# Sliding-window decode attention with an MLP: w4's first rows in eight loads, w3 in two, one more V quad moving

## The chip, the cores and the metric

The kernel runs on one core of one Trainium2 chip. The metric is the device time of one execution in microseconds (us); the time before is 194.92 us, the median of three runs. The profile is one execution of the same program, taken by the hardware profiler.

Engines: TensorE (PE; its weight loads are PEld), VectorE (DVE), ScalarE (ACT), GpSimd (POOL) and SyncE (SP). SP computes nothing; it issues the loads here. Sixteen DMA engines move the data.

## What is computed

Cut to what matters, for eight sequences of one token each:

```
x = A_x
def A(x):                                   # x: layer norm of A_x
    q = (x @ wq)                            # 32 heads of 128
    k = k_cache[:, :, SK - W:, :]           # W = 2048 of 8192 places, 8 kv heads
    v = v_cache[:, :, SK - W:, :]
    p = softmax(q k^T / sqrt(128))
    return (p v) @ wo
h = x + A(layernorm(x))
def Bf(y):                                  # y: layer norm of h
    x1 = y + 0                              # the token shift is zero for one token
    return x1 + gelu(layernorm(x1) @ w3) @ w4
out = h + Bf(layernorm(h))
```

wq and wo are 4 MB each in bf16, the windows of K and V 64 MB together, w3 (512 x 1792) and w4 (1792 x 512) 1.8 MB each. B_w1, B_w2 and B_x have no part in the result for one token, and no kernel here loads them.

## The kernel before

**The stream of loads.** SP issues all large loads through one helper, `dma` (L192 to L195; the instruction itself is at L194). The order is written out in `loads` (L282 to L289): wq, then for each sequence b ("row" b below, 0 to 7) two quads of K and, two rows behind, two quads of V, a quad being four kv heads, 2 MB; then four loads of wo, one of w3 and four of w4. K and V land in `ring`, eight slots of 16 KB in each of 128 partitions; a load waits until the quad that had its slot is used up. wo takes over the space of wq (`wbig`), w3 the ring's slot 0 and w4 slot 1 (`W3S`, `W4S`); their waits, `w_free`, are for the last transposes of K's quads in these slots. Each load raises a semaphore by 16, one step per DMA engine.

**Attention, row by row.** K is transposed on PE (L314), copied by ACT and DVE (L323, L325), multiplied with q (L334), and the softmax follows (L349 to L403). The product with V is made in quads, w = 2b + j for row b and half j; `i` counts quarter quads, i // 4 = w. `pe_PV` (L415) has two forms. In `moving` V is the moving operand, 4 matmuls of 512 columns for each i into one PSUM bank; after the fourth, DVE picks each head's own part in four instructions into `acc` (L446, L449), and `finish(w)` (L453) adds the parts with one matmul of `sum_f` (L456) and scales the result into `oT_all` (L412). In `held` V is the stationary operand, 16 matmuls of 16 columns for each i into `O_ps` (L430), and the result only needs scaling. Quads below NV = 14 are moving; the two quads of row 7 (w = 14 and 15) are held. `bank` gives quads 11 to 13 banks of their own. `turn` (L510) and `pv` (L515) fix where in PE's order the quarter quads and their `finish` stand.

**The end.** `reorder` (L486) brings the heads into wo's order, `pe_wo` (L499) multiplies with the four loads of wo, each behind its semaphore. Then h, its mean and variance (L598 to L612) and `uT`; `pe_w3` (L617) makes y = w3^T u, hidden index on partitions, in chunks of 128: chunks 0 to 7 into `y_ps[0]`, 8 to 13 into `y_ps[1]`, four matmuls each; `w4_chunks` says which rows of w4, and so which columns of w3, a chunk has. DVE scales y (L647), ACT applies gelu (L649), and `pe_w4` (L658, through `rows`, L652, matmuls at L654) adds h, as f_hi and f_lo, and the product with w4, group by group behind w4's four semaphores. ACT and DVE copy the result, SP stores it (L687).

The loads of w3 and w4 before:

```
584             B_w3.rearrange("(a p r) f -> p a (r f)", a=2, r=2), sem_w3, w_free[0])
...
587         w4_rows, w4_chunks = ((0, 4), (512, 4), (1024, 4), (1536, 2)), {}
...
593             dma(SP, w4_sb[:, lo:lo + r, :].rearrange("p r n -> p (r n)"),
594                 B_w4[f0:f0 + 128 * r, :].rearrange("(p r) n -> p (r n)", r=r), sem, w_free[1] if lo == 0 else None)
```

The first three loads of w4 bring 512 rows each, four neighbouring rows (4 KB) to each of 128 partitions; the fourth brings 256 rows, two to each.

Of the kernel before, what the change touches and what calls it, by code (L numbers as in the profile page):

```python
# [6 lines left out]
dt = mybir.dt  # L7
# [60 lines left out]
def bass_sequential_preLN__sliding_block_cached__mixer_s_mlp__decode_kernel(  # L68
# [23 lines left out]
    with es:  # L92
# [32 lines left out]
        w4_sb = ring[:, W4S, 0:FC * D].rearrange("p (k n) -> p k n", k=FC)  # L125
# [42 lines left out]
        g_x = sb([128, FC * B], dt.float32, "g_x")  # L168
        gT = sb([128, FC * B], dt.bfloat16, "gT")
# [18 lines left out]
        sem_x, sem_wq, sem_w3, sem_out = (S(n) for n in ("sem_x", "sem_wq", "sem_w3", "sem_out"))  # L188
# [111 lines left out]
        NV = 2 * (NB - 1)  # L300
# [104 lines left out]
        e_acc, e_oT = {}, {}  # L405

        def bank(w):
            return O_ps[:, :] if w < NV - 3 else kbank[(2, 3, 0)[w - NV + 3]]
# [6 lines left out]
        def pe_PV(i):  # L415
# [11 lines left out]
            def held(e):  # L427
                for c in range(16):
                    n = 16 * r + c
                    ins = e.matmul(O_ps[:, 16 * j:16 * (j + 1)], ring[:, s, n * DH:(n + 1) * DH],  # L430
                                   pT_sb[:, b % NB3, c, 64 * j + 16 * r:64 * j + 16 * (r + 1)],
                                   start=(n == 0), stop=(n == NCQ - 1))
                return ins

            if w >= NV:
                e_PV[i] = PE.op(held, landed(("v", b, j), r), e_pT[b, 3], e_acc[NV - 4])
                taken["v", b, j] = e_PV[i]
                return
            free = [e_xp[0]] if w == 0 else [e_acc[w - 1]] if w < NV - 3 else [e_lo[NG - 1], e_hi[NG - 1], e_lo[NG - 2], e_hi[NG - 2]]
# [46 lines left out]
        def reorder():  # L486
# [9 lines left out]
            e = PE.op(f, e_scale[LAST, 1], e_lo[NG - 1], e_hi[NG - 1], e_lo[NG - 2], e_hi[NG - 2])  # L496
# [17 lines left out]

        def pv(i):  # L515
            w = i // 4
            if i % 4 == 0 and 0 < w < NV - 3:
                finish(w - 1)
            pe_PV(i)
            if i % 4 == 0 and w == NV - 3:  # L520
                finish(w - 1)
            if i % 4 == 0 and w >= NV:
                for v in ((NV - 3, NV - 2), (NV - 1,))[w - NV]:
                    finish(v)
            if i == NG - 1:
                for j in range(2):
                    scale(LAST, j, O_ps[:, 16 * j:16 * (j + 1)], e_PV[i])
# [40 lines left out]
        for l in loads:  # L568
# [14 lines left out]
        dma(SP, w3_sb.rearrange("p (a r) f -> p a (r f)", a=2),  # L583
            B_w3.rearrange("(a p r) f -> p a (r f)", a=2, r=2), sem_w3, w_free[0])

        FH = 8
        w4_rows, w4_chunks = ((0, 4), (512, 4), (1024, 4), (1536, 2)), {}
        w4_ends = []
        for (f0, r), sem in zip(w4_rows, sem_w4):
            lo = len(w4_chunks)  # L590
            for i in range(r):
                w4_chunks[lo + i] = slice(f0 + i, f0 + 128 * r, r)
            dma(SP, w4_sb[:, lo:lo + r, :].rearrange("p r n -> p (r n)"),
                B_w4[f0:f0 + 128 * r, :].rearrange("(p r) n -> p (r n)", r=r), sem, w_free[1] if lo == 0 else None)
            w4_ends.append(lo + r)
        assert len(w4_chunks) == FC
# [20 lines left out]
        def pe_w3(lo, hi, *waits):  # L617
            def f(e):
                for fc in range(lo, hi):
                    n, f = divmod(fc, FH)  # L620
                    for kc in range(KC):
                        ins = e.matmul(y_ps[n][:, f * B:(f + 1) * B], w3_sb[:, kc, w4_chunks[fc]],
                                       uT[:, kc * B:(kc + 1) * B], start=(kc == 0), stop=(kc == KC - 1))
                return ins
            return PE.op(f, *waits)
        e_y = [pe_w3(0, FH, e_u, (sem_w3, 16), e_scale[LAST, 1]), pe_w3(FH, FC)]
# [12 lines left out]
        def bcf(t, n):  # L639
            a = t[:, :]  # L640
# [3 lines left out]
        for n in range(2):  # L644
            fn = (FH, FC - FH)[n]
            cs = slice(n * FH * B, (n * FH + fn) * B)
# [78 lines left out]
```

## Time and profile before

| | |
|---|---|
| runs | 194.76, 194.92, 195.19 us; median 194.92 |
| the profiled execution | 194.77 us; span from its first to its last instruction 193.0 us |
| PE, DVE, ACT busy | 81%, 53%, 43% of the span |
| read from HBM | 79.18 MB, 410 GB/s over the span |
| chain that ended last, by engine | DMA 56%, PE 33%, DVE 8% |
| SP's issues of w3 and w4 | five, from 158.79 to 175.24 us |
| clock granted to PE | full from 122.7 to 173.9 us, half from then on |

How to read the views. The page cuts the span into 40 equal slices of 4.8 us; a digit is the busy share of an engine in tenths, "DMA" the mean busy share of the 16 DMA engines, "GB/s" what they moved. The chain of waits goes back from the last instruction, at each step to what released it; a line has its start, its length and what it was. A table of stretches gives busy time and number of instructions per engine (PE, PEld, DVE, ACT, POOL), the granted clock, the DMA share and GB/s. A line of the timeline has start, length, engine, source line, operation, out<-in, shapes and number, and in brackets how long the engine stood idle before and what ended it. Besides these views the trace holds every step of every load's semaphore and one record for each DMA packet with its start, duration, size and queue.

### The profile page before, as it was taken

The numbers are of one execution on the slowest core, as the hardware profiler recorded it, in microseconds if no ns is written. First come the engines' busy times: TensorE is split into PE (matmuls) and PEld (weight loads), VectorE is DVE, ScalarE is ACT, GpSimd is POOL, SyncE is SP. The second block draws the span as 40 slices with busy tenths as digits, with TensorE's granted clock in tenths as the row PEclk, the third lists the DMA queues.
The fourth block names the chain that finished last, engine by engine and source line by source line (L and its number), as shares of the span: only waits on it lengthen the run. The fifth ranks groups of instructions, "written<-read, shape, count | busy, mean of one in ns | idle before, by whom it ended". The sixth has DMA issues, their size and how long they took to land.

```text
span 193.0 us, 4835 instructions
## 1 busy us (share of the span) xinstructions
PE 155.7 (81%) x2145; PEld 102.9 (53%) x2145; DVE 102.8 (53%) x256; ACT 82.7 (43%) x98; POOL 32.5 (17%) x40
## 2 busy tenths in 40 slices
PE   0028989889949999999789985999999798777753
PEld 0014767667736566566456643656565543347751
DVE  7702656456542665664756563464765735962051
ACT  5002866947822554464345442454445421430041
POOL 8000000350610080008000800044005200000000
PEclk9999999999996999999999998799999999995555
DMA  6999999999999999999999999999999999999981
GB/s 219 435 435 428 431 428 414 425 431 423 431 435 435 431 428 428 435 431 419 428 424 435 421 431 435 425 435 431 426 428 431 435 425 428 421 412 420 427 353 65
DMA packets 6740, 79.49 MB, mean 412 GB/s; under 512 B 688, under 2 KB 704, under 8 KB 2496
## 3 DMA queue, kind: packets, MB, share of 16 engines
q1 hardware_dynamic: 6704, 79.18, 96.8%
q8 instruction: 17, 0.28, 0.5%
q14 instruction: 3, 0.02, 0.0%
q10 hardware_dynamic: 16, 0.01, 0.0%
HBM read 79.18 MB, written 0.01 MB: 410 GB/s over the span
## 4 chain that ended last, share of the span: by engine, by line
DMA 56%; PE 33%; DVE 8%; issue 1%; SPq 1%; ACT 1%; ACTq 0%
DMA ring<-in_A_k_cache_dram 40%; PE kT_ps L314 13%; DMA ring<-in_B_w_dram 9%; PE O_ps L422 8%; DMA wbig<-in_A_wq_dram 6%; PE S_ps L334 4%; DVE acc L449 3%; PE S_ps L258 2%; DVE P_sb L371 1%; PE sm L456 1%; PE sm L381 1%; DVE iota_f L449 1%; DVE acc L446 1%; PE sm L400 1%; SPq L194 1%
## 5 line engine op out<-in xcount | busy, mean ns | idle before, releaser
L323 ACT ACTIVATE kT_sb<-kT_ps 128x1024 bf16<-128x1024 bf16 x64 | 65.2, 1024 | 66.4 <-PE kT_ps L314 66.4
L314 PE MATMUL kT_ps<-ident_p,ring 128*128 128x128 bf16 x1024 | 69.5, 222 | 7.9 <-DMA ring<-in_A_k_cache_dram 7.9
L325 DVE COPY kT_sb<-kT_ps 128x1024 bf16<-128x1024 bf16 x64 | 44.2, 691 | 51.7 <-PE kT_ps L314 51.6
L314 PEld LDWEIGHTS kT_ps<-ident_p,ring 128*128 128x128 bf16 x1024 | 59.2, 99 | 20.9 <-issue 10.2
L371 POOL TENSOR_TENSOR P_sb<-P_sb,mask_b 128x512 bf16<-128x512 bf16 x28 | 28.2, 1041 | 117.6 <-ACT P_sb L363 108.8
L422 PE MATMUL O_ps<-ring,pT_sb 128*64 128x512 bf16 x176 | 27.7, 402 | 0.0
L334 PE MATMUL S_ps<-kT_sb,qwin 128*32 128x512 bf16 x256 | 26.3, 395 | 0.0
L334 PEld LDWEIGHTS S_ps<-kT_sb,qwin 128*32 128x32 bf16 x256 | 6.8, 93 | 19.7 <-issue 17.7
L381 PE MATMUL sm<-ident_s,P_sb 128*128 128x128 bf16 x128 | 12.3, 219 | 3.8 <-DVE pT_sb L391 1.3
L391 DVE COPY pT_sb<-sm 128x512 bf16<-128x512 bf16 x28 | 11.7, 417 | 2.3 <-PE sm L381 2.3
L381 PEld LDWEIGHTS sm<-ident_s,P_sb 128*128 128x128 bf16 x128 | 8.1, 97 | 7.7 <-issue 3.7
L422 PEld LDWEIGHTS O_ps<-ring,pT_sb 128*64 128x64 bf16 x176 | 6.5, 109 | 4.6 <-issue 1.7
L449 DVE SCALAR_TENSOR_TENSOR acc<-O_ps,own_f,acc 128x128 f32<-128x128 f32 x24 | 8.4, 351 | 0.9
L363 ACT ACTIVATE P_sb<-S_ps,negcol 128x512 bf16<-128x512 f32 x8 | 5.5, 687 | 7.7 <-DVE negcol L362 7.7
L258 PE MATMUL S_ps<-wbig,xlnT 128*32 128x512 bf16 x32 | 3.6, 629 | 5.3 <-DMA wbig<-in_A_wq_dram 5.3
L456 PE MATMUL sm<-sum_f,acc 128*128 128x16 f32 x20 | 4.1, 281 | 3.6 <-DVE acc L449 1.6
L422 PE MATMUL kT_ps<-ring,pT_sb 128*64 128x512 bf16 x48 | 6.9, 388 | 0.0
L244 PE MATMUL sm<-ident_b,xln_b 8*128 8x8 bf16 x4 | 0.3, 174 | 7.5 <-DVE xln_b L217 7.5
L628 ACT ACTIVATE s<-vsum,eps 128x8 f32<-128x8 f32 x1 | 0.3, 302 | 13.9 <-DVE vsum L611 13.9
L345 DVE TENSOR_REDUCE mcol<-S_ps 128x1 f32<-128x512 f32 x8 | 5.5, 687 | 1.2 <-PE S_ps L334 1.2
L456 PEld LDWEIGHTS sm<-sum_f,acc 128*128 128x128 f32 x20 | 3.2, 200 | 5.1 <-DVE acc L449 2.6
L258 PEld LDWEIGHTS S_ps<-wbig,xlnT 128*32 128x32 bf16 x32 | 1.2, 138 | 6.8 <-issue 6.8
(113 smaller groups left out, 105.7 us busy)
## 6 DMA issues: line engine op xcount, KB each, us to landing
ring<-in_A_k_cache_dram SPq DMA_DIRECT2D x16, 2048.0 KB, 26.7
ring<-in_A_v_cache_dram SPq DMA_DIRECT2D x16, 2048.0 KB, 20.2
wbig<-in_A_wq_dram SPq DMA_DIRECT2D x1, 4096.0 KB, 12.2
wbig<-in_A_wo_dram SPq DMA_DIRECT2D x4, 1024.0 KB, 24.7
ring<-in_B_w_dram SPq DMA_DIRECT2D x1, 1792.0 KB, 26.9
ring<-in_B_w_dram SPq DMA_DIRECT2D x3, 512.0 KB, 17.7
ring<-in_B_w_dram SPq DMA_DIRECT2D x1, 256.0 KB, 17.8
x_sb<-in_A_x_dram ACTq DMA_DIRECT2D x1, 8.0 KB
```

Of the source, the lines that this page charges most:

```text
L258: ins = e.matmul(S_ps[u][32 * t:32 * (t + 1), :], xlnT[:, kc, :], wq_v[:, kc, lo:lo + 512], start=(kc == 0), stop=(kc == KC - 1), tile_pos ...
L314: ins = e.matmul(kT_ps[i % 2][:, c * 128:(c + 1) * 128], ring[:, s, n * DH:(n + 1) * DH], ident_p[:, :], is_transpose=True)
L323: e_lo[i] = AC.op(lambda e: e.activation(kT_sb[:, i % NKT, 0:1024], kT_ps[i % 2][:, 0:1024], ACT.Copy), e_Tlo[i], e_QK.get(i - NKT))
L325: e_hi[i] = DV.op(lambda e: e.tensor_copy(kT_sb[:, i % NKT, 1024:2048], kT_ps[i % 2][:, 1024:2048]), e_Thi[i], e_QK.get(i - NKT))
L334: ins = e.matmul(S_ps[b % 2][32 * h:32 * (h + 1), :], qwin[:, b, 4 * j + h, w0:w0 + 32], kT_sb[:, i % NKT, :].rearrange("p (c h k) -> p h ...
L345: e_max[b] = DV.op(lambda e: e.tensor_reduce(mcol[:, :], S_ps[b % 2][:, :], AX.X, ALU.max), e_QK[8 * b + 7], e_mT.get(b - 1))
L371: e_sp[b, r] = eng.op(lambda e, r=r, pb=pb, mb=mb: e.tensor_tensor(P4_sb[:, 128 * r:128 * (r + 1), :], pb, mb, ALU.mult), e_exp[b], e_PT.g ...
L381: ins = e.matmul(pT_ps[:, x * 128:(x + 1) * 128], P4_sb[:, 32 * c:32 * (c + 1), :].rearrange("p k h -> p (k h)"), ident_s[:, :], is_transp ...
L391: e_pT[b, r] = DV.op(lambda e: e.tensor_copy(dst, pT_ps[:, :]), e_PT[b, r], free)
L422: ins = e.matmul(bank(w)[64 * t:64 * (t + 1), :], pT_sb[:, b % NB3, c, 64 * j:64 * (j + 1)], ring[:, s, :].rearrange("p (a c d) -> p c a d ...
L449: e = DV.op(lambda e, own=own, src=src, dst=dst: e.scalar_tensor_tensor(dst, src, own, dst, ALU.mult, ALU.add), e)
L456: e_oT[w] = PE.op(lambda e: e.matmul(oT_ps[:, hh], acc[w % 3][:, :], sum_f[:, :], start=True, stop=True), e_acc[w], e_sum, small[0])
```

## The change

- **w4.** The first 512 rows go into partitions 0 to 63, eight neighbouring rows (8 KB) to each partition, by eight loads g = 0 to 7; load g brings the partitions g, g + 8, ... g + 56. All eight raise one semaphore, which is waited for at 128. The other three loads stay as they were. So w4 has 18 chunks instead of 14: eight of 64 rows (`FH` = 8 stays the border between the two banks of y) and ten of 128. `w4_sb` starts right behind w3 in the two slots of the ring, and all loads of w4 wait for `w_free[1]`.
- **w3.** Two loads of 256 rows, each with a semaphore. `pe_w3` runs first over all 18 chunks with the first half's rows (2 matmuls for each), then over chunks 0 to 7 and 8 to 17 with the second's.
- **w4's product.** The chunks of 64 rows use 64 partitions of gT and w4. `pe_fin` also waits for the scale of the last quad, which now has its result in the bank that `pe_fin` writes.
- **Row 7.** NV becomes 15: quad 14 is moving, into `O_ps`, and has its DVE instructions and a `finish`; quad 15 stays held, into `S_ps[1]`, and no longer waits for quad 10's DVE work. `at` and `late` write out where each `finish` stands: quad 11's goes from i = 56 to i = 54, quad 14's comes after i = 63, and `reorder` waits for it.

```
--- before.py
+++ after.py
...
-        w4_sb = ring[:, W4S, 0:FC * D].rearrange("p (k n) -> p k n", k=FC)
+        w34 = ring[:, W3S:W4S + 1, :].rearrange("p s n -> p (s n)")
+        w4_sb = w34[:, KC * F:KC * F + (FC + 4) * D].rearrange("p (k n) -> p k n", k=FC + 4)
...
-        g_x = sb([128, FC * B], dt.float32, "g_x")
-        gT = sb([128, FC * B], dt.bfloat16, "gT")
+        g_x = sb([128, (FC + 4) * B], dt.float32, "g_x")
+        gT = sb([128, (FC + 4) * B], dt.bfloat16, "gT")
...
-        sem_x, sem_wq, sem_w3, sem_out = (S(n) for n in ("sem_x", "sem_wq", "sem_w3", "sem_out"))
+        sem_x, sem_wq, sem_out = (S(n) for n in ("sem_x", "sem_wq", "sem_out"))
+        sem_w3 = [S(f"sem_w3{i}") for i in range(2)]
...
-        NV = 2 * (NB - 1)
+        NV = 2 * NB - 1
...
         e_acc, e_oT = {}, {}
+        OWN = {NV - 4: 2, NV - 3: 3, NV - 2: 0}
 
         def bank(w):
-            return O_ps[:, :] if w < NV - 3 else kbank[(2, 3, 0)[w - NV + 3]]
+            return kbank[OWN[w]] if w in OWN else O_ps[:, :]
...
                     n = 16 * r + c
-                    ins = e.matmul(O_ps[:, 16 * j:16 * (j + 1)], ring[:, s, n * DH:(n + 1) * DH],
+                    ins = e.matmul(S_ps[1][:, 0:16], ring[:, s, n * DH:(n + 1) * DH],
                                    pT_sb[:, b % NB3, c, 64 * j + 16 * r:64 * j + 16 * (r + 1)],
                                    start=(n == 0), stop=(n == NCQ - 1))
                 return ins
...
-                e_PV[i] = PE.op(held, landed(("v", b, j), r), e_pT[b, 3], e_acc[NV - 4])
+                e_PV[i] = PE.op(held, landed(("v", b, j), r), e_pT[b, 3])
                 taken["v", b, j] = e_PV[i]
                 return
-            free = [e_xp[0]] if w == 0 else [e_acc[w - 1]] if w < NV - 3 else [e_lo[NG - 1], e_hi[NG - 1], e_lo[NG - 2], e_hi[NG - 2]]
+            if w in OWN:
+                free = [e_lo[NG - 1], e_hi[NG - 1], e_lo[NG - 2], e_hi[NG - 2]]
+            else:
+                free = [e_xp[0]] if w == 0 else [e_acc[max(v for v in e_acc if v not in OWN)]]
             e_PV[i] = PE.op(moving, landed(("v", b, j), r), e_pT[b, r], *free)
...
-            e = PE.op(f, e_scale[LAST, 1], e_lo[NG - 1], e_hi[NG - 1], e_lo[NG - 2], e_hi[NG - 2])
+            e = PE.op(f, e_scale[LAST, 0], e_scale[LAST, 1], e_lo[NG - 1], e_hi[NG - 1], e_lo[NG - 2], e_hi[NG - 2])
...
+        at = {4 * (w + 1): (w,) for w in range(NV - 5)}
+        late = {4 * NV - 16: (NV - 5,), 4 * NV - 6: (NV - 4,), 4 * NV - 4: (NV - 3,), 4 * NV: (NV - 2,), NG - 1: (NV - 1,)}
+
         def pv(i):
-            w = i // 4
-            if i % 4 == 0 and 0 < w < NV - 3:
-                finish(w - 1)
+            for w in at.get(i, ()):
+                finish(w)
             pe_PV(i)
-            if i % 4 == 0 and w == NV - 3:
-                finish(w - 1)
-            if i % 4 == 0 and w >= NV:
-                for v in ((NV - 3, NV - 2), (NV - 1,))[w - NV]:
-                    finish(v)
             if i == NG - 1:
-                for j in range(2):
-                    scale(LAST, j, O_ps[:, 16 * j:16 * (j + 1)], e_PV[i])
+                scale(LAST, 1, S_ps[1][:, 0:16], e_PV[i])
+            for w in late.get(i, ()):
+                finish(w)
 
...
         w_free = [taken[quads[n - NS]] for n in (len(quads), len(quads) + 1)]
-        dma(SP, w3_sb.rearrange("p (a r) f -> p a (r f)", a=2),
-            B_w3.rearrange("(a p r) f -> p a (r f)", a=2, r=2), sem_w3, w_free[0])
-
-        FH = 8
-        w4_rows, w4_chunks = ((0, 4), (512, 4), (1024, 4), (1536, 2)), {}
+        for a, sem in enumerate(sem_w3):
+            dma(SP, w3_sb[:, 2 * a:2 * (a + 1), :].rearrange("p r f -> p (r f)"),
+                B_w3[256 * a:256 * (a + 1), :].rearrange("(p r) f -> p (r f)", r=2), sem, w_free[0])
+
+        w4_rows, w4_chunks = ((0, 64, 8), (512, 128, 4), (1024, 128, 4), (1536, 128, 2)), []
         w4_ends = []
-        for (f0, r), sem in zip(w4_rows, sem_w4):
+        for (f0, parts, r), sem in zip(w4_rows, sem_w4):
             lo = len(w4_chunks)
-            for i in range(r):
-                w4_chunks[lo + i] = slice(f0 + i, f0 + 128 * r, r)
-            dma(SP, w4_sb[:, lo:lo + r, :].rearrange("p r n -> p (r n)"),
-                B_w4[f0:f0 + 128 * r, :].rearrange("(p r) n -> p (r n)", r=r), sem, w_free[1] if lo == 0 else None)
-            w4_ends.append(lo + r)
-        assert len(w4_chunks) == FC
+            w4_chunks += [(parts, slice(f0 + i, f0 + parts * r, r)) for i in range(r)]
+            dst = w4_sb[0:parts, lo:lo + r, :].rearrange("p r n -> p (r n)")
+            rows_in = B_w4[f0:f0 + parts * r, :].rearrange("(p r) n -> p (r n)", r=r)
+            step = 128 // parts * 4 if parts < 128 else 1
+            for g in range(step):
+                dma(SP, dst[g::step], rows_in[g::step], sem, w_free[1])
+            w4_ends.append((len(w4_chunks), 16 * step))
+        FH = w4_ends[0][0]
+        NCH = len(w4_chunks)
...
-        def pe_w3(lo, hi, *waits):
+        def pe_w3(half, lo, hi, *waits):
             def f(e):
                 for fc in range(lo, hi):
-                    n, f = divmod(fc, FH)
-                    for kc in range(KC):
-                        ins = e.matmul(y_ps[n][:, f * B:(f + 1) * B], w3_sb[:, kc, w4_chunks[fc]],
-                                       uT[:, kc * B:(kc + 1) * B], start=(kc == 0), stop=(kc == KC - 1))
+                    parts, rows_of = w4_chunks[fc]
+                    n, f = (0, fc) if fc < FH else (1, fc - FH)
+                    for kc in (2 * half, 2 * half + 1):
+                        ins = e.matmul(y_ps[n][0:parts, f * B:(f + 1) * B], w3_sb[:, kc, rows_of],
+                                       uT[:, kc * B:(kc + 1) * B], start=(kc == 0 and f == 0), stop=(kc == KC - 1),
+                                       skip_group_check=True)
                 return ins
             return PE.op(f, *waits)
-        e_y = [pe_w3(0, FH, e_u, (sem_w3, 16), e_scale[LAST, 1]), pe_w3(FH, FC)]
+        pe_w3(0, 0, NCH, e_u, (sem_w3[0], 16), e_scale[LAST, 1], e_acc[NV - 2])
+        e_y = [pe_w3(1, 0, FH, (sem_w3[1], 16)), pe_w3(1, FH, NCH)]
...
-        def bcf(t, n):
-            a = t[:, :]
+        def bcf(t, n, ps):
+            a = t[ps, :]
             return bass.AP(tensor=a.tensor, offset=a.offset, ap=[a.ap[0], [0, n], [1, B]])
 
         e_gT = []
         for n in range(2):
-            fn = (FH, FC - FH)[n]
-            cs = slice(n * FH * B, (n * FH + fn) * B)
-            e = DV.op(lambda e, n=n, cs=cs, fn=fn: e.tensor_tensor(v3(g_x[:, cs]), v3(y_ps[n][:, 0:fn * B]), bcf(r2, fn),
-                                                                   ALU.mult), e_y[n], e_r2)
-            e_gT.append(AC.op(lambda e, cs=cs: e.activation(gT[:, cs], g_x[:, cs], ACT.Gelu_apprx_tanh), e))
+            fn = (FH, NCH - FH)[n]
+            ps, cs = slice(0, w4_rows[n][1]), slice(n * FH * B, (n * FH + fn) * B)
+            e = DV.op(lambda e, n=n, ps=ps, cs=cs, fn=fn: e.tensor_tensor(
+                v3(g_x[ps, cs]), v3(y_ps[n][ps, 0:fn * B]), bcf(r2, fn, ps), ALU.mult), e_y[n], e_r2)
+            e_gT.append(AC.op(lambda e, ps=ps, cs=cs: e.activation(gT[ps, cs], g_x[ps, cs], ACT.Gelu_apprx_tanh), e))
...
-                    ins = rows(e, [gT[:, fc * B:(fc + 1) * B]] * KC,
-                               [w4_sb[:, fc, cols[nb]] for nb in range(KC)],
-                               stop=(fc == FC - 1))
+                    p = slice(0, w4_chunks[fc][0])
+                    ins = rows(e, [gT[p, fc * B:(fc + 1) * B]] * KC,
+                               [w4_sb[p, fc, cols[nb]] for nb in range(KC)],
+                               stop=(fc == NCH - 1))
...
-        PE.op(pe_fin, e_fin, e_exp[LAST])
-        pe_w4(0, w4_ends[0], (sem_w4[0], 16), e_gT[0])
-        pe_w4(w4_ends[0], w4_ends[1], (sem_w4[1], 16))
-        pe_w4(w4_ends[1], w4_ends[2], (sem_w4[2], 16), e_gT[1])
-        e_z = pe_w4(w4_ends[2], w4_ends[3], (sem_w4[3], 16))
+        PE.op(pe_fin, e_fin, e_exp[LAST], e_scale[LAST, 1])
+        for n, (hi, count) in enumerate(w4_ends):
+            e_z = pe_w4(w4_ends[n - 1][0] if n else 0, hi, (sem_w4[n], count), e_gT[min(n, 1)])
```

## The prediction

> **What bounds the kernel now.** I read the 40 slices first, to see which resource is full, then the chain of waits, then stretches of the tail.
>
> ```profile
> PE   0028989889949999999789985999999798777753
> DMA  6999999999999999999999999999999999999981
> GB/s 219 435 435 428 431 428 414 425 431 423 431 435 435 431 428 428 435 431 419 428 424 435 421 431 435 425 435 431 426 428 431 435 425 428 421 412 420 427 353 65
> ```
>
> Transfers are at a ceiling of 435 GB/s in nearly every slice; only the last but one falls to 353. The chain of waits says what ends last:
>
> ```profile
> 171.72 17.66 DMA ring<-in_B_w_dram
> 189.37 0.04 issue
> 189.42 0.60 PE S_ps L654 x12
> 190.02 0.01 issue
> 190.03 0.41 PE S_ps L654 x6
> 190.44 0.02 issue
> 190.47 0.31 ACT P_sb L682
> ```
>
> The third and fourth load of w4 are the last waits: 16 matmuls follow the one, 8 (0.41 us) the other, then copies and the store. The stretches of the tail (busy time per engine, clock, share of the 16 DMA engines, GB/s) show how these loads end:
>
> ```profile
> 185.60:187.00 1.40, 1.21 (x37) 1.25 (x38) 0.65 (x4) 0.70 (x1) 0.00 (x0) 0.50 0.95 375
> 187.20:188.70 1.50, 1.50 (x58) 1.40 (x55) 0.26 (x2) 0.50 (x2) 0.00 (x0) 0.50 0.57 232
> 188.90:189.50 0.60, 0.09 (x10) 0.08 (x12) 0.00 (x0) 0.00 (x0) 0.00 (x0) 0.50 0.50 195
> ```
>
> A share of 0.57 is nine engines of 16, 0.50 is eight: seven are done before 187.2, one more before 188.9. The trace has the time of every one of the 16 steps by which a load's semaphore rises, one per DMA engine:
>
> ```
> load     seven engines    one engine   eight engines
> w3       182.57-182.91    184.45       184.16, 185.44-185.65
> w4 1st   183.81-184.14    185.73       186.69-186.92
> w4 2nd   185.09-185.41    186.94       187.90-188.14
> w4 3rd   186.37-186.62    188.21       189.15-189.37
> w4 4th   186.96-187.26    188.84       189.79-189.98
> ```
>
> Why eight are late: the page has 17 packets of 16 KB on the instruction queue. Within an engine each packet record starts some 4 ns before the last one's end, so the 16 chains can be followed. The 16 fetches up to 184.7 fall on eight engines in turn, twice each, and each sets its engine back about 1.4 us (0.95 until the next data packet, and 0.47 on that packet: 1,079 ns against 611). The single engine was hit by two 8 KB fetches (44.2, 139.2). The eight packets of the load of x, the only load of eight rows, lie on the engines without 16 KB fetches: the seven and the single one.
>
> **The change, part by part.** Against the profiled run: 194.77 us, span 193.0, 1.77 around it; the median of the runs is 194.92, 0.15 above.
>
> *Eight loads of w4.* Eight rows go to eight engines, one 8 KB packet each, and if they are the engines of x, the late eight lose 32 KB each and the other eight carry 64 KB instead of 32. Starts of neighbouring packets are 607 ns apart at 16 KB, 268 at 7 KB, 155 at 4 KB: on that line 8 KB is 306, and a closing 4-byte record adds 6. So 8 x 0.312 = 2.49 us instead of 8 x 0.155 + 0.006 = 1.25. The late engines end at 189.98 - 1.25 = 188.73. The single engine ends at 188.84 + 1.25 = 190.09: 0.11 later than all did before. The seven would end at 187.26 + 1.25 = 188.5, were nothing in their way.
>
> *What may be in their way* is new: eight engines write into half the partitions, eight partitions apart at a time. No row shows it. Lower bound of the stretch, 1: each engine writes at its own rate, as the 16 do in loads over all partitions (16,384 B in 607 ns, 27 GB/s). Upper bound: the store at the end, also eight rows on eight engines, from eight adjacent partitions. Its packets of 1,024 B take 44, 74, 71, 44, 44, 60, 60 and 44 ns, the long ones overlapping others; together 8 KB in 160 ns, 51 GB/s, 4.2 times less than 8 x 27. So the price for the seven lies between 0 and 3.2 x 2.49 = 8.0 us. A packet that overlaps another takes up to 1.7 times 44 though overlapped in part only; I take a stretch of 2, engines in pairs, since here the partitions are spread over 64 and not adjacent. Then: landing of w3 on the seven (middle 182.7) + 4.98 + 3.13 (their middle from w4's first load to its last, 183.95 to 187.08) = 190.8, less 0.1 because the engines of a pair are 0.0 to 0.3 apart: 190.7. That passes the single engine's 190.09, and is **0.72 us behind** 189.98. The single engine, 1.75 us behind its partner, is past the overlap.
>
> [...]
>
> *SP's queue.* Five issues become 13. Those of L194 that waited for nothing took 0.44 to 0.60 us, so eight more cost at most 4.8 us: the last ends at 180.0 instead of 175.24, and its first packet is due when the seven reach it, at 186.0 or later. Hidden by 6 us of queued loads; without them each would cost its 0.5. Only the store stands behind them on SP.
>
> *w3 in two loads, w3's matmuls in halves.* The first half (36 matmuls: 18 chunks x 2) runs from 183.85, when uT is there, in the 2.0 us in which PE waited for the whole of w3:
>
> ```profile
> 185.79 1.95 PE L622 MATMUL kT_ps<-uT,ring 128*128 128x8 bf16 x56 [2.02 <-DVE xb L634]
> 187.84 1.07 PE L654 MATMUL S_ps<-ring,gT 128*8 128x128 bf16 x32
> 189.42 0.99 PE L654 MATMUL S_ps<-ring,gT 128*8 128x128 bf16 x24 [0.52 <-DMA ring<-in_B_w_dram]
> ```
>
> At 1.95 / 56 = 35 ns, 36 matmuls behind the second half's landing (185.65) end at 187.0, not 187.74: PE gains 0.7 us. The 18 chunks of w4 are 72 matmuls instead of 56: 16 x 33 ns = 0.53 more, ahead of the last two loads and covered by their wait (0.8 before the third now). End to end 0.
>
> *Row 7's first quad moving.* Four groups of 16 held matmuls (0.56 + 1.80 for five) become four of 4 with 512 columns (1.05 for two groups), and four DVE instructions, one matmul pair and a scale follow:
>
> ```profile
> 169.92 1.05 PE L422 MATMUL kT_ps<-ring,pT_sb 128*64 128x512 bf16 x8
> 170.91 0.56 PE L430 MATMUL O_ps<-pT_sb,ring 128*128 128x16 bf16 x16
> 171.40 1.13 DVE L449 SCALAR_TENSOR_TENSOR acc<-kT_ps,own_f,acc 128x128 f32<-128x128 f32 x3
> 172.96 1.80 PE L430 MATMUL O_ps<-pT_sb,ring 128*128 128x16 bf16 x64
> 176.87 0.41 PE L492 MATMUL kT_ps<-oT_all,ident_p 128*32 128x64 bf16 x16 [0.40 <-DVE oT_all L412]
> 181.40 1.02 PE L504 MATMUL S_ps<-oR,wbig 128*128 128x8 bf16 x32 [0.80 <-DMA wbig<-in_A_wo_dram]
> ```
>
> 171.0 + 2.1 + 0.4 for finish(12) = 173.5; with the second quad 176.1; finish(14) and its scale, 0.59 + 0.23, end near 177.0, where the scales now end at 176.8. So 0.2 later, behind it the reorder and three loads of wo; the fourth wo load, at 181.35, holds PE 0.80 us there and covers it. Without that cover it costs 0.2.
>
> Sum: +0.72 for the loads, 0 for the rest: 195.5 against the profiled run, **195.6** against the median.
>
> **The rivals.** *No sharing (not slower).* The seven end at 188.5, the late at 188.73, but the single engine decides, at 190.09, because it was 1.1 us ahead of the late ones and takes on 1.25. +0.1: 195.0. For it: 16 engines write side by side now without loss. Against: the store's packets. It holds while the stretch stays under 1.63 (182.9 + 1.63 x 2.49 + 3.13 = 190.09).
>
> *The single engine is not among the eight, and no sharing.* Then no load lands after 188.73 and PE ends the kernel: w3 done at 187.0, 0.35 for f_hi and f_lo, 72 x 33 ns = 2.4: 189.75 instead of 190.44. -0.69: 194.2. Against: the chain with the fetch at 44.2 starts with a packet of x.
>
> *The eight loads fall on the late engines:* 189.98 + 1.25, 196.2. Against: the same chains. A stretch of 3 or more (over 198) is counted here.
>
> **How the numbers follow.** Sharing in pairs 0.50, no sharing 0.28, no single engine 0.14, the last 0.08. 0.2% is 0.39 us, about what a measurement of this kernel tells from no change. A stretch of 1.63 to 1.74 would still be within it (0.03 of the first case). So faster 0.15, within 0.31, slower 0.54. The first case alone gives 195.2 to 195.9; the range 194.2 to 196.2 takes in the first three and stops short of a stretch of 3.
>
> **What would show it.** Sharing: packets of 8 KB near 600 ns instead of 310, the first w4 loads complete on the seven at 187.5, DMA share near 1 until 187, and the last landing near 190.7. No sharing: packets of 310 ns and a DMA share of about 0.06, one engine, from 188.8 to 190.1. PE after the last landing still takes 0.4. The matmuls of w3 should stand in two groups, from 183.9 and 185.7, and PE should still wait for the fourth load of wo. I am wrong if the last landing of w4 comes before 189.6, or if PE ends later than 0.6 us after it.

## The result, and the profile after

The changed kernel takes 200.31 us (median of five runs, 199.78 to 200.95) against 194.92 before: a ratio of 1.0275, 95% interval 1.0249 to 1.0301. The profiled execution has a span of 198.1 us instead of 193.0. The direction was forecast, the size was not: 0.7 us were forecast and 5.4 came.

The page of the changed kernel, busy tenths and GB/s in 40 slices (here of 4.95 us):

```profile
PE   0028979889949996999999949999999888886773
DMA  6999999999999999999999999999999999999950
GB/s 220 443 417 433 430 427 430 420 432 430 430 433 427 420 430 430 437 437 425 424 420 437 420 440 440 424 427 420 432 420 440 433 430 421 409 418 415 246 164 16
```

The line of DMA is the trap of this profile: in the third slice from the end the digit is still 9, at 246 GB/s, and in the next it is 5, at 164. A packet counts as busy for as long as it lasts: from 183 to 185 us, below, the packets' time is 1.02 of the sixteen engines' at 229 GB/s. The end of the chain of waits (start, length, what):

```profile
175.27 19.19 DMA ring<-in_B_w_dram
194.46 0.04 issue
194.50 0.60 PE S_ps L664 x15
195.11 0.41 PE S_ps L664 x6
195.55 0.31 ACT P_sb L691
```

As before, w4's third and fourth loads land last, at 194.46 and 195.07, and 0.4 us of PE follow. The fourth load landed at 189.98 before, so the 5.1 us are all in the landings. Stretches of the tail, the changed kernel (busy time per engine, clock, DMA share, GB/s):

```profile
181.00:182.50 1.50, 0.83 (x31) 0.83 (x32) 0.00 (x0) 0.00 (x0) 0.00 (x0) 0.50 1.04 424
183.00:185.00 2.00, 1.12 (x5) 1.02 (x6) 1.22 (x8) 0.22 (x2) 0.00 (x0) 0.50 1.02 229
185.00:187.00 2.00, 2.00 (x19) 1.98 (x20) 1.34 (x7) 1.55 (x3) 0.00 (x0) 0.50 0.99 218
187.00:189.00 2.00, 1.60 (x28) 1.51 (x28) 0.00 (x0) 0.00 (x0) 0.00 (x0) 0.50 0.92 266
```

Two of these stretches in the kernel before:

```profile
183.00:185.00 2.00, 0.76 (x4) 0.63 (x3) 1.24 (x8) 0.49 (x2) 0.00 (x0) 0.50 1.04 430
185.00:187.00 2.00, 1.21 (x37) 1.25 (x38) 1.18 (x7) 1.28 (x1) 0.00 (x0) 0.50 0.94 372
```

The rate falls to half at about 182.9 us, 0.6 us after the first packet of the eight loads starts (182.28), at an unchanged DMA share. The packet records say whose packets are slow: everyone's. Duration in ns of one packet that starts

```
                                  before 182.7   183.3-184.2   184.8-184.9   187.3-187.7
8 KB, the eight loads of w4       309            622-647       392-407       309-472
7 KB, w3, the late engines        272            558-580       360-375
4 KB, w4's second load            159            319-335       185-236       159-162
```

From 183.3 to 184.2 all three sizes are stretched by the same factor, 2.0 to 2.1. From 188.2 to 189.6 the 4 KB packets are at 271 to 330 again.

One more difference stands in PE's timeline: w3's matmuls, two groups of 36.

```profile
184.91 2.78 PE L630 MATMUL kT_ps<-uT,ring 128*64 128x8 bf16 x36 [0.88 <-DVE hc L619]
188.10 2.82 PE L630 MATMUL kT_ps<-uT,ring 128*64 128x8 bf16 x36 [0.40 <-DMA ring<-in_B_w_dram]
```

They take 77 ns each on average instead of 35. They end at 190.9, well before the last landing, and so cost nothing here, but they matter below.

### The profile page after: what moved, and what is told of

Same layout as the page of the kernel before. It is cut to its first block, busy times and chain, and to the rows that moved or that the text cites. A ratio compares the mean times of both kernels' runs of the same rounds, so it can differ in the third digit from the quotient of the medians.

```text
span 198.1 us, 4819 instructions
## 1 busy us (share of the span) xinstructions
PE 160.4 (81%) x2131; PEld 106.0 (54%) x2131; DVE 104.1 (53%) x260; ACT 82.7 (42%) x98; POOL 32.5 (16%) x40
## 4 chain that ended last, share of the span: by engine, by line
DMA 49%; PE 29%; SPq 12%; DVE 5%; ACT 2%; issue 1%; POOL 1%; ACTq 0%
DMA ring<-in_A_k_cache_dram 39%; PE kT_ps L316 14%; SPq L196 12%; DMA ring<-in_B_w_dram 10%; PE O_ps L425 7%; PE S_ps L336 4%; DVE kT_sb L327 1%; PE sm L383 1%; PE sm L462 1%; DVE iota_f L455 1%; DVE acc L455 1%; PE sm L351 1%; ACT L365 1%; DVE mcol L347 1%; POOL P_sb L373 1%
## 5 line engine op out<-in xcount | busy, mean ns | idle before, releaser
L425 PE MATMUL O_ps<-ring,pT_sb 128*64 128x512 bf16 x192 | 29.8, 400 | 0.0
L425 PEld LDWEIGHTS O_ps<-ring,pT_sb 128*64 128x64 bf16 x192 | 7.3, 109 | 5.1 <-issue 1.3
L630 PE MATMUL kT_ps<-uT,ring 128*128 128x8 bf16 (+1 forms) x72 | 5.6, 213 | 1.3 <-DVE hc L619 0.9
L630 PEld LDWEIGHTS kT_ps<-uT,ring 128*128 128x128 bf16 (+1 forms) x72 | 5.4, 160 | 1.5 <-DVE hc L619 1.0
```

The source lines that it names most:

```text
L425: ins = e.matmul(bank(w)[64 * t:64 * (t + 1), :], pT_sb[:, b % NB3, c, 64 * j:64 * (j + 1)], ring[:, s, :].rearrange("p (a c d) -> p c a d ...
L630: ins = e.matmul(y_ps[n][0:parts, f * B:(f + 1) * B], w3_sb[:, kc, rows_of], uT[:, kc * B:(kc + 1) * B], start=(kc == 0 and f == 0), stop= ...
```

## The experiments

Runs of one group shared their runs of the kernel before, 194.85 to 194.92 us. Ratios are to these, with 95% intervals; they can differ by up to 0.2% from the quotient of the medians. "Last landing" is that of w4 in the profiled execution, in us.

| run | what lies in w4's first group | us | ratio | last landing |
|---|---|---|---|---|
| the change | eight loads, partitions 8 apart | 200.31 | 1.0275 (1.0249-1.0301) | 195.07 |
| e1_w4_as_before | as before; the rest of the change | 194.84 | 0.9991 (0.9982-1.0001) | 189.95 |
| e2_w4_alone | eight loads; the rest as before | 200.54 | 1.0279 (1.0259-1.0300) | 194.78 |
| e3_one_load | one load, partitions 0-63 | 198.40 | 1.0194 (1.0161-1.0227) | 193.31 |
| e4_four_loads | four loads, partitions 4 apart in 0-63 | 197.80 | 1.0139 (1.0115-1.0163) | 192.06 |
| e5_low_and_high | two loads, 0-31 and 64-95 | 197.82 | 1.0152 (1.0138-1.0166) | 192.73 |
| e6_low_only | two loads, 0-31 and 32-63 | 199.49 | 1.0242 (1.0228-1.0256) | 193.92 |
| e7_all_8k | one load, all 128, 8 KB each | 194.80 | 0.9990 (0.9975-1.0005) | 190.11 |
| e8_eight_distinct | eight loads, 4 apart, 0-31 and 64-95 | 198.09 | 1.0165 (1.0151-1.0179) | 193.32 |
| e9_even | one load, partitions 0, 2, ... 126 | 196.26 | 1.0067 (1.0044-1.0090) | 190.02 |
| e10_own | eight loads, 4 apart in 0-31 or 32-63 | 196.34 | 1.0072 (1.0046-1.0098) | 191.09 |
| e11_upper | as e10 in 64-95 or 96-127 | 200.45 | 1.0287 (1.0260-1.0314) | 195.65 |
| e12_own_half | as e10, half the bytes | 195.58 | 1.0031 (1.0014-1.0048) | 190.50 |
| e13_own_32col | as e10, w3 in 32-column matmuls | 196.25 | 1.0075 (1.0056-1.0094) | 191.19 |
| e14_four_engines | eight loads of four partitions | 196.01 | 1.0056 (1.0043-1.0069) | 190.53 |
| e15_six_engines | eight loads of six partitions | 196.23 | 1.0072 (1.0060-1.0084) | 191.38 |

### Which part of the change

**e1_w4_as_before** takes the eight loads away and keeps the rest:

```
-w4_rows, w4_chunks = ((0, 64, 8), (512, 128, 4), ...
+w4_rows, w4_chunks = ((0, 128, 4), (512, 128, 4), ...
```

> The whole change except the eight loads: the first 512 rows of w4 come in one load over 128 partitions, as before; w3 in halves and row 7's first quad moving stay. If the eight loads alone cost the 5.4 us, whichever way they do it, this is within 0.3 us of the kernel before, 194.6 to 195.2, with the last landing of w4 near 190.0. If the split of w3 or row 7 has a part in it, it is 196 or more.

It took 194.84 us, 0.9991 of before. Together, w3 in halves and row 7's moving quad are worth nothing and cost nothing. PE's timeline in this run shows the gain that went nowhere:

```profile
183.70 1.07 PE L630 MATMUL kT_ps<-uT,ring 128*128 128x8 bf16 x28
185.72 1.07 PE L630 MATMUL kT_ps<-uT,ring 128*128 128x8 bf16 x28 [0.95 <-DMA ring<-in_B_w_dram]
189.40 0.98 PE L664 MATMUL S_ps<-ring,gT 128*8 128x128 bf16 x24 [0.64 <-DMA ring<-in_B_w_dram]
```

w3 is done at 186.8 instead of 187.7, and PE then waits for the same landing as before.

**e2_w4_alone** is the counterpart: the kernel before with w4's rows, loads and 18 chunks from the change, w3 in one load (`sem_w3`, one `pe_w3` group for each bank) and NV = 14.

> The kernel before with only the eight loads of w4 (18 chunks); w3 in one load, row 7 held. If the eight loads cost it all: 199.8 to 200.8, packets of 8 KB near 620 ns and those of every engine stretched by about 2. If the half loads of w3 are needed for the stretch (7 KB packets on all engines at once with the 8 KB ones): under 198.

200.54 us, 1.0279: the eight loads, with their 18 chunks, cost it all. This run also ends theory P (below), since PE reads nothing of w3 until all of it has landed, at 188.34, while the rate is already down:

```profile
183.00:185.00 2.00, 0.80 (x4) 0.66 (x4) 1.21 (x8) 0.46 (x2) 0.00 (x0) 0.50 1.07 246
185.00:187.00 2.00, 0.00 (x0) 0.00 (x0) 1.21 (x7) 1.31 (x2) 0.00 (x0) 0.50 0.97 223
```

PE's busy time is 0.00 from 185 to 187, and 223 GB/s are moved.

### What about these loads is slow

Three theories stood here: W, the writes into few partitions; R, the reading of rows that lie evenly apart; P, PE's reading of w3 next to the writes. **e3_one_load** brings the same rows to the same 64 partitions in one load, **e4_four_loads** in four.

```
-step = 128 // parts * 4 if parts < 128 else 1
+step = 1                                           # e3
+step = 128 // parts * 2 if parts < 128 else 1      # e4
```

> The changed kernel with the same 64 partitions and rows in one load, 64 packets of 8 KB over sixteen engines, four each. Theory W (the writes into few partitions at a time stretch the packets of all engines, and half the partitions have half the way in): 512 KB take up to 2.5 us instead of 1.25, 195.3 to 196.4. Theory R (eight rows 64 KB apart read in step): no such step here, 194.8 to 195.3. Theory P (PE's reading of w3 in 64-column slices disturbs the writes next to it): PE's work is that of the changed kernel, so 199.5 or more.

> The same 512 rows in four loads of sixteen partitions (g, g + 4, ... g + 60), sixteen packets of 8 KB each, one per engine. Theory W with twice the places per load: as the one load, 195.3 to 196.4. Theory R: sixteen rows 32 KB apart in step, 198 or more. If it is only that eight engines carry twice their share, which this undoes: 194.8 to 195.3. Theory P: 199.5 or more.

198.40 and 197.80 us: no theory had these sizes. W was nearest in kind, but 512 KB at half the rate would have cost 1.25 us, and 3.5 and 2.9 came. The stretches of e3 say why:

```profile
183.00:185.00 2.00, 1.40 (x10) 1.30 (x9) 1.23 (x8) 0.48 (x2) 0.00 (x0) 0.50 0.95 225
185.00:187.00 2.00, 2.00 (x32) 1.98 (x32) 1.20 (x7) 1.29 (x2) 0.00 (x0) 0.50 1.05 244
187.00:189.00 2.00, 1.14 (x15) 1.05 (x12) 0.00 (x0) 0.00 (x0) 0.00 (x0) 0.50 1.01 223
```

The rate of all engines together is halved for six microseconds, not for the 2.5 that this load would need. While the early engines write into the 64 partitions, the late ones' packets of w3, which go to all 128, last 480 ns on average (those that start from 183 to 187 us) instead of 272.

**e7_all_8k** keeps the packets of 8 KB and gives up the half of the partitions.

```
-w4_rows, w4_chunks = ((0, 64, 8), (512, 128, 4), (1024, 128, 4), (1536, 128, 2)), []
+w4_rows, w4_chunks = ((0, 128, 8), (1024, 128, 4), (1536, 128, 2)), []
```

> The first 1024 rows of w4 in one load of 8 KB to each of 128 partitions, then 512 and 256 rows; w4 in three loads and 14 chunks. It has the packets of 8 KB without the half of the partitions. Theory W1 and W2: no stretch, 194.6 to 195.4, 8 KB in 309 ns. If packets of 8 KB from w4, or their reading, are at fault: 197 or more.

194.80 us, 0.9990, and every 8 KB packet in 309 ns. So it is not the size of the packets. Where they are written is the other difference from e3, beside the rows of each load; e9 to e11 below keep the rows and change the partitions alone.

### Which partitions

**e6_low_only** and **e5_low_and_high** load 32 partitions at a time and differ in one number, the start of the second 32. w3's columns are taken in two matmuls of 32 and gelu is done in two parts, so that both have the same work.

```
+BASES, STEP = (0, 64), 1       # e5; e6: (0, 32), e8: (0, 64), 4
...
+for base in BASES:
+    dst = w4_sb[base:base + 32, lo:lo + r, :]...
+    dma(SP, dst[g::step], rows_in[g::step], sem, w_free[1])
```

> The control to the one before: the same two loads of 32 partitions, 0 to 31 and 32 to 63, the same work on PE. Both theories: as the one load of 64 partitions, 198.0 to 199.0, every engine's packets stretched from about 182.9 us. If it comes near 195, it was the form of that one load and not its partitions.

> The first 512 rows of w4, 8 KB to a partition, in two loads of 32 partitions, 0 to 31 and 64 to 95; all else as in the changed kernel (w3's columns and gelu follow the partitions). Theory W1: what counts is how many partitions are written, 64 instead of 128. Then it is as the one load of 64, 198.0 to 199.0. Theory W2: partitions have their ways in by number, partitions 0 to 63 share half of them, and 0 to 31 with 64 to 95 reach all: no stretch, 194.6 to 195.4, packets of 8 KB near 309 ns throughout. [...]

199.49 and 197.82 us. The partitions' numbers matter (1.7 us between two runs that differ in them alone), so W1 falls; but e5 isn't free either, which W2 had wanted: its grouping of the partitions was a supposition, and no run shows it. **e8_eight_distinct** goes back to eight loads, each into partitions four apart.

> Eight loads of eight partitions again, but of partitions four apart: 0 + g, 4 + g, ... 28 + g and 64 + g, ... 92 + g for g = 0 to 3. Theory W2: each of eight engines has a way of its own, no stretch: 194.2 to 195.2, as the cases without sharing in the prediction. Theory W1 (few partitions at a time): as the changed kernel, 199.5 to 200.8. If eight rows read in step from places that lie evenly apart are at fault: 198 or more.

198.09 us, and between the 195 of W2 and the 200 of W1. Both misses have one thing in common: the expectation asked whether the engines of one load meet each other, not whether they meet the engines of another load that is running at the same time. The packet records of e8 show a stretch that all engines have at once, whatever they load, and that swings:

```
start us         182.2-182.7   183.6      184.3      184.6      185.1-185.2
8 KB packets     309 ns        556-567    384-385    549-559    391-395
7 KB packets     272 ns        485-489    319-346    501-513    340-358
```

At each moment both sizes are stretched by about the same factor, between 1.2 and 1.9. So whatever holds up the packets of one load holds up those of the other. e10 and e11 below suggest why it swings: e8's loads go by turns into the partitions of e10's first four loads, where nothing is stretched, and into those of e11's first four, where everything is. In the changed kernel all sixteen packets under way at 183.9 us are stretched: 319 to 335 ns at 4 KB, 558 to 574 at 7 KB, 635 to 647 at 8 KB.

### Has each engine its own way in?

Theory O, a supposition, puts this together: in a load over 128 partitions each of the sixteen engines has a way of its own into the partitions that it writes, and the stretch comes where two engines meet on one way. Which partitions a load of eight must then take to keep to its engines' own ways, no trace shows: the packet records have no engine numbers. The author assumed eight that are four apart in the lower half. **e10_own** takes these and changes nothing else:

```
-dma(SP, dst[g::step], rows_in[g::step], sem, w_free[1])
+lanes = slice(None) if step == 1 else slice(32 * (g // 4) + g % 4, 32 * (g // 4 + 1), 4)
+dma(SP, dst[lanes], rows_in[lanes], sem, w_free[1])
```

> The changed kernel with other partitions in each of the eight loads: load g brings partitions 32a + b, 32a + b + 4, ... 32a + b + 28 (a = g // 4, b = g % 4), so partitions four apart within 0 to 31 or 32 to 63; the same 64 partitions, rows, sizes and work of PE. Theory O (in a load over 128 partitions each engine has its own way in, and no two use one; the eight loads' engines keep to their own when the eight partitions of a load are four apart in the lower half, and the stretch comes where two engines meet on one way): no stretch, 8 KB in 309 ns throughout, 194.2 to 195.2, as the two cases without sharing in the prediction. Theory F (loads of fewer than 128 partitions stretch every engine's packets, wherever they write): 198 or more. [...]

**e11_upper** reads exactly the same rows in the same order and writes them 64 partitions higher.

```
-dst = w4_sb[0:parts, lo:lo + r, :].rearrange("p r n -> p (r n)")
+dst = w4_sb[128 - parts:128, lo:lo + r, :].rearrange("p r n -> p (r n)")
```

> As the one before, but written into partitions 64 to 127, four apart within 64 to 95 or 96 to 127; the product still reads partitions 0 to 63, so the output leaves out these rows of w4. [...] Theory O: stretch for as long as the late engines have work, 197.5 to 200.5. [...] Theory F: 198 or more.

196.34 and 200.45 us. e10's time misses theory O's range (more on this below), but its packets do what the theory said. First e10's stretches, then e11's:

```profile
183.00:185.00 2.00, 1.92 (x13) 1.78 (x13) 1.11 (x9) 0.35 (x2) 0.00 (x0) 0.50 1.00 409
185.00:187.00 2.00, 2.00 (x32) 1.97 (x32) 1.32 (x7) 1.42 (x2) 0.00 (x0) 0.50 0.94 381
```

```profile
183.00:185.00 2.00, 1.09 (x6) 0.98 (x6) 1.14 (x8) 0.30 (x2) 0.00 (x0) 0.50 0.99 203
185.00:187.00 2.00, 2.00 (x20) 1.98 (x21) 1.34 (x7) 1.47 (x2) 0.00 (x0) 0.50 1.00 211
```

409 against 203 GB/s, from the destination alone. In e10 every packet of 8 KB lasts 309 ns, every one of 7 KB 272 but for two behind an instruction fetch. Theories R and F (any load of few partitions stretches) fall with this pair: the reading is the same in both, and both load eight partitions at a time. What the pair shows is that the partitions decide. That it is by two engines meeting on one way is theory O's reading: it fits every run here, but no record shows the ways, and a load that holds up the others by leaving its engines' own ways, met or not, would look the same.

**e9_even** asks the same of one load of 64 partitions spread over all 128.

```
-dst = w4_sb[0:parts, lo:lo + r, :].rearrange("p r n -> p (r n)")
+dst = w4_sb[0:128:128 // parts, lo:lo + r, :].rearrange("p r n -> p (r n)")
```

> The 64 partitions 0, 2, 4, ... 126 in one load of 64 packets of 8 KB over sixteen engines; the product still reads partitions 0 to 63, so the output leaves out part of w4's first 512 rows. Theory F: as the one load into partitions 0 to 63, 198 to 199. Theory O: the partitions lie on all ways, so no stretch (194.6 to 195.4) if each engine gets the rows of its own way, and some, up to 198, if the rows are dealt out in another order than in a load of 128.

No stretch, 309 ns throughout, and the last landing at 190.02, as before. That 64 partitions are half of 128 doesn't matter, then; e3 reads the same rows in one load too, and differs in the partitions alone. Theory O had this outcome for the case that each engine gets the rows of its own way; which rows each got is not on record. The time is still 1.4 us longer, by PE:

```profile
183.83 5.55 PE L630 MATMUL kT_ps<-uT,ring 128*64 128x8 bf16 x72
189.62 2.19 PE L664 MATMUL S_ps<-ring,gT 64*8 64x128 bf16 x72
```

w3's 72 matmuls take 5.55 us without a gap, and PE ends at 191.8, 1.4 us later than before.

**e12_own_half** is e10 with packets of 4 KB, from which theory O and the forecast's set of engines promised the fastest kernel of all.

```
+w4_rows, w4_chunks = ((0, 64, 4), (256, 128, 4), (768, 128, 4), (1280, 128, 4)), []
```

> The loads of partitions four apart with half the bytes: the first 256 rows of w4, four to a partition, eight packets of 4 KB in each of eight loads; then 512, 512 and 512 rows (16 chunks). Theory O: the late engines end 0.62 us earlier (189.36) and the single engine 0.62 later (189.46), so the last landing is 0.5 us earlier than before and the time 194.2 to 194.6, the fastest here. Theory F: a stretch over half the time, 196 to 198.

195.58 us, 1.0031. There is no stretch, but the last landing is 190.50 and not 189.46. That is near 189.98 + 0.62: a late engine got 16 KB more to do, not less. The next part finds them.

### The 1.5 us that stay in e10

e10's 196.34 us are 1.5 more than before (one expectation below has 1.3). Two things are late in it: the last landing, and PE.

The landings first. Each engine goes through w3's second load, the small loads if it has any, and w4's other three loads in this order (before, the first seven steps of w3 come at 182.57 to 182.91, those of w4's loads at 183.81 to 184.14, 185.09 to 185.41, 186.37 to 186.62 and 186.96 to 187.26), so the steps of two semaphores, matched by their times, tell which engines had the small loads. Before, the early engines took from 182.74 to 187.1 for all of w4 (middles of their steps), 4.4 us; without the first load's 1.25 that is 3.1 to 3.2, with eight packets of 8 KB (2.49) on top 5.6 to 5.7.

```
step of w3's 2nd load     small loads   should end at    step of w4's 4th load
182.43-182.84             no            185.6-186.0      185.68, 185.73         2 engines
182.43-183.26             yes           188.0-189.0 }
185.28-185.86             no            188.4-189.1 }    188.09-188.94          10 engines
184.01                    no            187.1-187.2      187.35                 1 engine
184.46                    yes           190.1-190.2      190.10                 1 engine
185.28-185.86             yes           190.9-191.6      191.09, 191.09         2 engines
```

Seven engines had their step of w3 by 183.26; two of them are without the small loads, so five have them, besides the single engine and two late ones: eight. **e14_four_engines** and **e15_six_engines** load four and six partitions at a time, to see which of the eight the late ones are.

```
+BASES, STEP, WD = (0, 32), 4, 16       # e14; e15: 24
+w4_rows = ((0, 32, 8), (256, 128, 4), (768, 128, 4), (1280, 128, 4))      # e14
+w4_rows = ((0, 48, 8), (384, 128, 4), (896, 128, 4), (1408, 128, 3))      # e15
...
+dst = w4_sb[base:base + WD, lo:lo + r, :]...
```

> Eight loads of four partitions (four apart: 0 + b to 12 + b and 32 + b to 44 + b), 8 KB each: 256 rows of w4 on four engines, then 512, 512 and 512 rows over 128 partitions; w4 reaches into the ring's slot 2, and the 32 partitions take matmuls of 16 columns. Each of the four engines gets 64 KB more and 16 KB less, all others 16 KB less (0.62 us). If a load of fewer rows takes the first of the same eight engines and the two late ones are not among the first four: last landing 189.4 if the single engine isn't either (194.2 to 194.6, the fastest), 190.7 if it is (195.5 to 195.9). If a late one is among the four: 191.9 and 196.6 or more.

> As the one before with six partitions to a load: 384 rows of w4 on six engines, 64 KB more and 24 KB less each (1.56 us), all others 24 KB less (0.93 us); 19 chunks. If the two late engines are the seventh and eighth: last landing 190.4, the single engine's, if it is among the six (195.1 to 195.6), or 189.1 (194.0 to 194.4) if not. If a late one is among the six: 191.5 and 196.2 or more. Steps of the first of these loads' semaphores on how many early engines tell which.

The last landing of e14 is 190.53 (190.7 expected with the single engine among the four and no late one), with nothing else after 189.3; e15's is 191.38 (191.5 expected with a late one among the six). Read against w3's steps as above, the four are three early engines and the single one, the six add an early and a late one, the eight another early and another late one. e15's time, 196.23, is as expected from its landing; e14's, 196.01, is above the 195.5 to 195.9 that went with its own: PE has a wait of 1.74 us there in which the profile shows no releaser.

Now PE. In e10 it is busy without a gap from w3's first matmul to its last instruction, at 191.97:

```profile
183.99 5.55 PE L631 MATMUL kT_ps<-uT,ring 128*64 128x8 bf16 x72
189.78 2.19 PE L665 MATMUL S_ps<-ring,gT 64*8 64x128 bf16 x72
```

**e13_own_32col** is e10 with two matmuls of 32 columns for each of 64, as in e5 and e6, to separate PE's part.

> The eight loads of partitions four apart (no stretch there, yet 1.3 us slower than before), with w3's product for the rows in partitions 0 to 63 in two matmuls of 32 columns each instead of one of 64. Reading S: of the 1.3 us, 1.1 is two late engines among the eight (last landing 191.09 instead of 189.98) and the rest PE, whose 72 matmuls of w3 took 5.55 us, 77 ns each instead of 35, and left it busy until 191.97. Then here PE has 3.6 to 4.0 us for w3, ends 0.4 behind the last landing, and the time is 195.6 to 195.9. If the matmuls of 64 columns are no slower in themselves but are held up by the writes: as the one it is made from, 196.1 to 196.4.

196.25 us, no faster than e10 within the intervals. By its time alone that would be the second reading, matmuls held up by the writes; but beside the same writes w3 now takes 3.93 us for 104 matmuls, 38 ns each, so they were slow in themselves. The time went elsewhere, as the chain of waits shows:

```profile
188.16 0.91 PE S_ps L677 x26
189.07 1.34 issue
190.41 1.46 PE S_ps L677 x46
```

w4's second load had landed at 189.33, and PE went on at 190.41; the profile names no releaser for the 1.1 us between, and their cause stays open. A 16 KB fetch on the instruction queue ran from 188.05 to 188.93, and e13 has 32 matmuls more than e10, so a wait for code is possible, but it is not shown. So PE's share of e10's 1.5 us isn't measured as a difference of times. From the traces: PE ends 1.56 us later in e10 than before (190.41). A last landing at 191.09 and the usual 0.4 behind it would let PE end at 191.5, so the two late engines alone would have cost 1.1. But PE's own work alone costs nearly all of it, since e9, whose landings are on time, ends at 191.8. The two overlap: in e10 the late landings are hidden behind PE.

No run here beats the kernel before; e1 and e7 are as fast.

## Why the prediction was right in direction and wrong in size

Landings first, since the sum was one of landings: 189.98 before, 190.7 forecast, 195.07 measured. Of the 5.1 us, 4.0 are the stretch (195.07 to e10's 191.09) and 1.1 the set of engines (191.09 to 189.98).

- **The step that failed: "What may be in their way".** Its stretch of 2 was about the right factor for an 8 KB packet (622 to 647 ns; 600 forecast), in part by luck: it was argued from pairs within a load, while the packets of all loads were stretched alike. It was charged to the wrong bearers. The sum put 2 x 2.49 us on the seven early engines and then let all engines go on at full rate: "their middle from w4's first load to its last" at 3.13, the late engines at 188.73. Instead all sixteen ran at half rate from 182.9 to 187 and again from 188, with the late engines' w3 and w4 in it. e10 and e11 show that the partitions written are the cause; that engines make everyone wait by writing on ways that others use at the time is the reading that fits all runs, and no record shows the ways. Sharing in pairs within a load, which was forecast, may add to it; no run shows it.
- **The bound was there, the range wasn't.** The store's packets allowed up to 8.0 us for the seven engines, and the forecast said so. But it thought of the price only as longer packets of the eight loads: above 196.2 it had only a stretch of 3 or more, within a chance of 0.08 shared with another case. No packet of the eight was stretched by 3; the others' packets were stretched too, and that was in no case. (Its threshold of 1.63 starts from the last of the seven, 182.9, and its sum from their middle less 0.1; from there the threshold would be 1.75. Nothing hangs on it.)
- **The set: "if they are the engines of x".** Wrong for two of the eight, and 1.1 us of the last landing by itself (e10). It rested on chains of packets followed over 180 us, in which packets of several engines start within a few ns of each other. The tail alone, with the small packets as marks, gives the set without that. Whether the load of x lies on other engines or the chains had swapped stays open. "The eight loads fall on the late engines" was listed with all eight in mind; two suffice, since the last one decides.
- **The rivals.** No sharing is what e10 has (309 ns, as that case said), but not on this kernel's partitions. With no sharing the last landing was to be 190.09; e10's single engine has 190.10, and the two late ones spoil it.
- **SP's queue, row 7, w3 in halves.** Forecast at 0. e1, with the halves and row 7, has 0.9991. The eight small issues, which e1 lacks, take 0.56 to 0.70 us each in the changed kernel; SP's last issue ends at 176.2, 6 us before the first of these packets starts.
- **w3's matmuls.** "At 1.95 / 56 = 35 ns" was carried to a form that the trace had not shown. With 40 matmuls of 128 columns at 36 ns (35 before, 38 in e1), the 32 of 64 columns take (5.55 - 1.44) / 32 = 128 ns. It is hidden in the changed kernel and costs up to 1.4 us where the landings are on time (e9).

## What to carry to other kernels

A load into a part of the partitions isn't cheap because it is small: here it could slow every transfer in flight to half, by the choice of its partitions alone (203 GB/s in e11, 409 in e10). To shift bytes from one engine to another, try which partitions leave the other packets as they are: here eight at a time, four apart in 0 to 31 or 32 to 63 (e10, 8 KB in 309 ns), did. Look at the packets' durations, not at the DMA share, which stayed at 0.92 to 1.02 in the changed kernel from 183 to 189 us, at 218 to 266 GB/s. Before counting on idle engines, find out which ones a small load gets: a marked packet in the tail (another size) shows it in one run. And a slice of weights of another width or stride is another instruction: its price is not that of its neighbour (128 ns against 36 in e10's w3).

## What the runs showed of the hardware

- Loads into part of the partitions can slow all sixteen engines, by about the same factor at the same moment (1.2 to 1.9 in e8; 2.0 to 2.1 in the changed kernel from 183.3 to 184.2 us), down to 203 to 246 GB/s of 430 (e11, e2); the same rows in other partitions don't (409 in e10). Meeting on a way is the reading that fits; no record shows it.
- The price of a matmul with its weights depends on their form. Time of one w3 matmul with its weights: 128 columns at a step of 4 or 2 elements 35 to 38 ns; 128 columns at a step of 8, (1.50 - 12 x 0.036) / 16 = 67 ns (e7, 28 matmuls in 1.50 us); 64 columns at a step of 8, 128 ns (e10); 64 columns at a step of 4, (2 x 1.54 - 48 x 0.036) / 16 = 85 ns (e12); 32 columns at a step of 8, (3.93 - 1.44) / 64 = 39 ns (e13). The weight loads' own durations in the changed kernel, from the groups of PE's weight loads (min / median / max ns):

```profile
L630 PEld LDWEIGHTS kT_ps<-uT,ring x72: 103/118/217, 184.9 to 190.7; 128*128 128x128 bf16 x40, 128*64 128x64 bf16 x32
```

- In the changed kernel the semaphore of the eight loads of eight partitions has eight records from 170.82 to 175.17, one per issue, and 64 from 183.09 on, as the packets land, and the wait for 128 is met. The records give no amounts; by an estimate from these counts an issue raises it by eight.
